# Moving three sets of halved matmuls between chunks, and four VectorE sums to an earlier place, in a fused attention and feed-forward kernel

## The chip, the core and the metric

The kernel runs on one core of a Trainium2 chip. The time is device time in microseconds, the median of several executions. Of the kernel before, 8 executions are known: 280.6 to 282.26 us, median 281.54.

## The reference

A linear attention over 8 batches of 576 tokens with 8 heads of 64 gives 4608 tokens of 512 numbers; a feed-forward layer with a hidden width of 2048 follows.

```python
def _attn_ref(q, k, v):                       # (8, 8, 576, 64) each
    ...
    q_p, k_p = phi(q, cos_w, sin_w), phi(k, cos_w, sin_w)     # relu, times cos and times sin of the position
    kv = np.einsum('bhsf,bhsd->bhfd', k_p, v)
    z = np.sum(k_p, axis=2)
    num = np.einsum('bhsf,bhfd->bhsd', q_p, kv)
    den = np.einsum('bhsf,bhf->bhs', q_p, z)[..., None] + 1e-06
    return (num / den).astype(np.float32)

def _moe_ref(x, w_in, w_out, beta):           # x: (4608, 512)
    h = x @ w_in                              # (4608, 2048)
    g = h * (1.0 / (1.0 + np.exp(-beta * h)))
    return (g @ w_out).astype(np.float32)
```

## The kernel before

The feed-forward part goes over nine chunks (c = 0 to 8) of 512 tokens. For each chunk TensorE forms the hidden values in 16 tiles of 128 (jt), ScalarE takes the swish of each from PSUM into g_t, and TensorE multiplies by w_out. The attention of batch b = c + 1 is laid between the matmuls of chunk c, so that its result (xs, turned by a DMA transpose into xt) is there for the chunks behind. While chunk c runs, the inputs of the next batches are loaded and prepared as well: k_relu and v_scale (on VectorE or ScalarE), q_relu, a DMA transpose of q (q_turn_dma) and q_tan on GpSimd.

Everything is issued in an order written out by hand: each engine executes its instructions in the order in which the code records them, and semaphores keep the engines together. TensorE's list is one straight program. A matmul stands in it as two instructions, a weight load and the matmul itself, which reads up to 512 columns.

Two pieces of the attention are made of very small matmuls, and each of them stands as one unbroken block among the large ones:

- kv_mm (L266, matmul on L272), for both halves of the heads: 72 matmuls of 130 columns, in each chunk up to 6.
- num_mm (L286, matmul on L293), called through num_all (L328) for the three parts of a batch: 144 matmuls of 65 columns. In chunk 1 it is called at slot 18 (one_unit, L818), in chunks 2 to 4 behind h_first (L984), in chunks 5 and 6 at the entry N0 of ORDER.

How the matmuls of the feed-forward part are formed differs from chunk to chunk:

- Chunks 0 and 1: h_group (L410: h_mm, then h_act) for the 16 hidden tiles, then o_part (L530) for the output, four slots for each of four token tiles. o_part has a parameter cols: with 2, each of its matmuls but the very first of a tile is issued as two of half the columns. In chunk 1 this holds for slots 24 to 31 (L833).
- Chunks 2, 3 and 4: h_first (L950) makes the hidden tiles with h_group. The output comes from o_fast (L533): two halves, x and y, of seven products each ("1" to "7"), put together from sums of the g tiles (S1 to S4) and of the weights (T1 to T4) with additions on VectorE (a2, a3, a7) and copies on ScalarE (c1, c5, cu, c4). Each product is eight matmuls of 256 columns; with its last argument set, the last seven are issued as two of 128.
- Chunks 5 to 8: chunk() (L885) walks a list of names, ORDER (L843) for chunks 5 and 6, ORDER_END for 7 and 8. Half of the hidden tiles come in pairs (X, Y, Z, V) from h_fast (L463) in seven products of two matmuls, and eight come plainly as p0 to p7 from h_plain (L419), which also takes cols. Before, H_COLS halves p0 to p7 of chunk 6, and O_COLS halves six of the fourteen output products of chunk 5 (x: 4; y: 2, 5, 7, 3, 4). Both are on L857.

h_fast needs four sums of x, t1 to t4 in the tile wx["x"]. For chunks 6 and later they are the entries t1 to t4 of the lists; for chunk 5 they are made by x_sums (L454) at the end of chunk 4 (L1019), by VectorE. In chunk 4 the end of the code is: y5, c5, v_half, y6, cu, y2, a2, v_half, y7, a7, v_half, y3, a3, v_half, x_sums, v_half, y4, c4. The sums need xt of chunk 5, of which the last part comes from batch 5 (x_part, L992).

Of the kernel before, what the change touches and what calls it, by code (L numbers as in the profile page):

```python
# [16 lines left out]
P = 128  # L17
# [5 lines left out]
def kernel(  # L23
# [14 lines left out]
    nc = tc.nc  # L38
# [5 lines left out]
    MI = DM // P  # L44
# [3 lines left out]
    NB = TCH // 64  # L48
    HP = P // 2
# [319 lines left out]
    def h_bank(c, jt):  # L369
        if c < 2 and jt < 4:  # L370
            return ((3, 2, 5, 0), (6, 7, 4, 5))[c][jt]
        return ((6, 7, 4, 5) if c == 0 else (0, 1, 4, 5))[jt % 4]

    def h_mm(c, jt, mis=range(4), blocks=slice(0, NB)):
        xt = xt_tile(c)
        for mi in mis:
            jp, g = divmod(mi, 2)
            nc.tensor.matmul(ps[:, h_bank(c, jt), blocks.start * 64 : blocks.stop * 64],  # L378
                             lhsT=win[jt // 4][:, mi, (jt % 4) * P : (jt % 4 + 1) * P],
                             rhs=xt[:, blocks, jp, g * HP : (g + 1) * HP],  # L380
                             start=(mi == 0), stop=(mi == MI - 1 and blocks.stop == NB))

    def h_act(c, jt):
        if (c, jt // 4) not in gs:
# [22 lines left out]
        nc.vector.tensor_tensor(T2[:, a], B22[:, a], T1[:, a], op=z)  # L407
        nc.vector.tensor_tensor(T4[:, a], B21[:, a], T2[:, a], op=z)

    def h_group(c, jt):  # L410
        h_mm(c, jt)
        h_act(c, jt)

    def h_silu(c, jt, bank):
# [115 lines left out]
    def o_part(c, tt, part, cols=1):  # L530
        o_mm(c, tt, range(4 * part, 4 * part + 4), cols)

    def o_fast(c, pr, banks, cols=""):  # L533

        b_ps, e_ps, a_ps = (ps[:, k_, 0:HM] for k_ in banks)
        tok = slice(pr * P, (pr + 1) * P)
        last = c == NTC - 1 and pr == 1

        def prod(dst, left, right, start, stop, pieces=False):
            order = (0, 1, 2, 3, 4, 5, 7, 6) if c + 1 >= B else range(JT // 2)  # L540
            for i in order:
                w = HM // 2 if i and pieces else HM
                for m in range(0, HM, w):
                    nc.tensor.matmul(dst[:, m : m + w], lhsT=left(i), rhs=right[:, i, m : m + w],  # L544
                                     start=start and i == 0,
                                     stop=stop and i == order[-1], skip_group_check=True)

        def g_part(r, hf):
            def at(i):
                jt = 2 * i + r  # L550
                return gs[c, jt // 4][:, jt % 4, hf * (TCH // 2) + pr * P : hf * (TCH // 2) + (pr + 1) * P]
            return at

        def s_part(t):
            return lambda i: t[:, i, tok]

        o1 = osb_pool.tile([P, DM], FP32, name="o_sb", tag="o_sb")
        o2 = osb_pool.tile([P, DM], FP32, name="o_sb", tag="o_sb")
        p1 = part.tile([P, HM], FP32, name="p1", tag="p1")
        p5 = part.tile([P, HM], FP32, name="p5", tag="p5")  # L560
        u = part.tile([P, HM], FP32, name="u", tag="u")

        def c4():
            h = HM // 2 if last else HM
            nc.scalar.copy(o2[:, 0:h], b_ps[:, 0:h])
            if last:
                nc.vector.tensor_copy(o2[:, h:HM], b_ps[:, h:HM])
                store(c, pr + 2, o2, 0, HM)

        def stored(key, op):  # L570
            def do():
                op()
                waits[key[0]].discard(key[1:])
                if not waits[key[0]] and not (last and key[0] == "2"):
                    store(c, pr + (2 if key[0] == "2" else 0), o2 if key[0] == "2" else o1)
                if last and key == "2a7":
                    store(c, pr + 2, o2, HM, DM)
            return do

        waits = {"1": {"a2", "a3"}, "2": {"a7", "c4"}}  # L580
        add = dict(op=ALU.add)
        return {
            "1": lambda: prod(b_ps, g_part(0, 0), B11, True, False, "1" in cols),
            "5": lambda: prod(e_ps, s_part(S1), T1, True, False, "5" in cols),
            "6": lambda: prod(b_ps, s_part(S2), T2, False, False, "6" in cols),
            "2": lambda: prod(a_ps, g_part(1, 0), B21, True, True, "2" in cols),
            "7": lambda: prod(b_ps, s_part(S3), T3, False, False, "7" in cols),
            "3": lambda: prod(e_ps, s_part(S4), B22, False, True, "3" in cols),
            "4": lambda: prod(b_ps, g_part(1, 1), T4, False, True, "4" in cols),
            "c1": lambda: nc.scalar.copy(p1, b_ps),  # L590
            "c5": lambda: nc.scalar.copy(p5, e_ps),
            "cu": lambda: nc.scalar.copy(u, b_ps),
            "c4": stored("2c4", c4),
            "a2": stored("1a2", lambda: nc.vector.tensor_tensor(o1[:, 0:HM], a_ps, p1, **add)),
            "a3": stored("1a3", lambda: nc.vector.tensor_tensor(o1[:, HM:DM], e_ps, u, **add)),  # L595
            "a7": stored("2a7", lambda: nc.vector.tensor_tensor(o2[:, HM:DM], b_ps, p5, **add)),
        }
# [231 lines left out]
    for slot in range(32):  # L829
        if slot < 16:  # L830
            h_group(1, slot)
        else:
            o_part(1, (slot - 16) // 4, slot % 4, 2 if slot > 23 else 1)  # L833
        one_unit(slot)

    def k_piece(b, j):
# [20 lines left out]
    H_COLS, O_COLS = {6: 8}, {5: ("4", "25734")}  # L857

    def x_sum(c, kind):
        xt, n = xt_tile(c), NB // 2  # L860
# [24 lines left out]
    def chunk(c, b, x, y, parts):  # L885
# [27 lines left out]
        for op in (ORDER if b < B else ORDER_END).split():  # L913
            n = int(op[-1]) if op[-1].isdigit() else None
            if op == "K":
                kv_mm(b, 0, 4)
                kv_mm(b, 1, 4)
            elif op == "kt":
                kv_take((0, 1), 4)
            elif op[0] == "N":  # L920
                for t, bank in enumerate(parts):
                    num_all(b, t, bank)
            elif op[0] == "x":
                x_part(b, n, parts[n])
                take(op)
            elif op[0] in "kvwq":
                take(op)
            elif op[0] == "t":
                if c + 1 < NTC:
                    x_sum(c + 1, n)  # L930
            elif op[0] == "g":
                if b + 1 < B:
                    q_tan(b + 1, n, None if n else last_sum)
            elif op[0] == "p":
                h_plain(c, plain[n], plain_bank(n), 2 if n < H_COLS.get(c, 0) else 1)
            elif op[:2] == "sp":
                h_silu(c, plain[n], plain_bank(n))
            elif op[0] == "o" and n is not None:
                outs[op[1]][op[2]]()
            elif op[0] == "o":  # L940
                outs[op[2]]["a" + op[1]]()
            elif op[0] == "c" and op[2] in "xyo":
                outs["x" if op[2] == "o" else op[2]][op[:2]]()
            elif op[0] == "s":
                last_sum = g_sum(c, 2 * int(op[1]), 2 * int(op[1]) + 2, n)
            else:
                pair = op[0] if op[0] in pairs else op[-1]
                pairs[pair][op.replace(pair, "")]()

    def h_first(c):  # L950
        b = c + 1
        for slot in range(16):
            h_group(c, slot)
            if c == 2:
                if slot == 0:
                    wx_tiles()
                    k_all(b)
                    v_half(b, 1)
                if slot == 3:
                    att_q(b + 1)  # L960
                if slot == 5:
                    nc.vector.tensor_tensor(T3, B22, B12, op=ALU.subtract)
            if slot == (10 if c == 2 else 1):
                kv_all(b)
            if slot in (3, 7, 11):
                g_sums(c, slot // 2 - 1, slot // 2 + 1)
            elif slot in (13, 15):
                sums = g_sums(c, slot // 2, slot // 2 + 1)
            if c == FAST - 1 and slot in (2, 4, 6, 8, 10, 12):
                wh_sums((0, 4, 8, 12, 2, 6)[slot // 2 - 1])  # L970
        return sums

    FAST = 5
    for c in range(2, NTC):
        b = c + 1
        parts = (6, 0, 4) if c < FAST else (0, 6, 4)
        cols = O_COLS.get(c, ("", ""))
        xb, yb = ((2, 3, 6), (1 if c == FAST - 1 else 7, 3, 6)) if c < FAST else ((3, 2, 0), (1, 2, 0)) if b < B else ((0, 3, 6), (1, 3, 6))
        x, y = o_fast(c, 0, xb, cols[0]), o_fast(c, 1, yb, cols[1])
        if c >= FAST:  # L980
            chunk(c, b, x, y, parts)
            continue
# [21 lines left out]
        v_half(b + 1, 0, 0, 3)  # L1004
        y["5"]()
        y["c5"]()
        v_half(b + 1, 1, 2, 3, "act")
        y["6"]()
        y["cu"]()
# [6 lines left out]
        y["3"]()  # L1016
        y["a3"]()
        v_half(b + 1, 0, 7, 9)
        if c == FAST - 1:  # L1019
            x_sums(c + 1)  # L1020
        v_half(b + 1, 1, 3, 9, "act")
        y["4"]()
        y["c4"]()
# [30 lines left out]
```

## Time and profile before

| what | us |
|---|---|
| median of 8 executions | 281.54 (280.6 to 282.26) |
| the profiled execution | 282.26 |
| its span, first to last instruction | 280.5 |
| TensorE busy | 270.9 |
| VectorE, ScalarE, GpSimd busy | 209.6, 177.9, 71.9 |
| matmuls of num_mm in a chunk, first to last start: chunks 1, 2, 3 | 1.79, 1.68, 2.45 |
| the same, chunks 4, 5, 6 | 1.24, 1.31, 1.30 |

A row of the profile's table of groups gives the line, the engine, the operation, what it writes and reads, how often, the busy time and the mean of one, and then the idle time of the engine before it and what ended most of it ("<-"). "issue" there means that the engine waited for nothing that the profile shows. The chain in order of time gives for each step the start, the length, the engine, the tile and line, and the number of instructions. Durations of single matmuls in the profile overlap, so where it matters the time from one start to the next is used. The granted clock of TensorE is full (1.00) in every ten microseconds but the last (0.91).

### The profile page before, as it was taken

To read this page: it belongs to the slowest core of one execution; us is meant where nothing else is said; L and a number is where in the kernel's file an instruction comes from. 1 tells how busy PE (TensorE), PEld (TensorE's weight loads), DVE (VectorE), ACT (ScalarE), POOL (GpSimd) and SP (SyncE) were. 2 spreads that over 40 slices of the span, in tenths; PEclk is the share of its full clock that TensorE was granted. 3 is DMA by queue.
4 is the path that set the end of the run, shared out by engine and by line. 5 is a ranking of instruction groups with operands and counts; after the bars stand their busy time and mean duration, and the time that the engine had idled before them with its cause. 6 is when DMAs were issued, how large, how long until landed. Compare 5 with 4: busy or idle time off the path is not lost.

```text
span 280.5 us, 8681 instructions
## 1 busy us (share of the span) xinstructions
PE 270.9 (97%) x3586; PEld 192.1 (68%) x3592; DVE 209.6 (75%) x539; ACT 177.9 (63%) x348; POOL 71.9 (26%) x89
## 2 busy tenths in 40 slices
PE   8899999999999999998999999999999999999993
PEld 8454455454674588547854786679888886888783
DVE  5889977659999586356749977799679779649832
ACT  5778856772137557674857585896586169529911
POOL 1444000624194074106320452008400140000000
PEclk9999999999999999999999999999999999999998
DMA  7999999989979959993899189507400540033006
GB/s 235 384 393 380 393 389 299 361 231 398 177 226 324 309 144 255 130 378 52 215 205 367 31 192 229 211 3 119 120 1 5 124 112 1 2 75 78 0 2 150
DMA packets 50583, 53.98 MB, mean 192 GB/s; under 512 B 31200, under 2 KB 31472, under 8 KB 50544
## 3 DMA queue, kind: packets, MB, share of 16 engines
q1 hardware_dynamic: 47584, 45.82, 58.0%
q0 software_dynamic: 2688, 7.34, 9.5%
q8 instruction: 28, 0.46, 0.7%
q10 hardware_dynamic: 272, 0.27, 0.4%
q14 instruction: 11, 0.09, 0.1%
HBM read 36.71 MB, written 9.44 MB: 165 GB/s over the span
## 4 chain that ended last, share of the span: by engine, by line
PE 90%; DMA 3%; DVE 3%; issue 1%; SPq 1%; ACTq 0%; ACT 0%
PE ps L544 30%; PE ps L378 24%; PE ps L472 11%; PE ps L521 10%; PE ps L426 7%; PE ps L293 4%; DMA raw_v<-in_v_dram 3%; PE ps L272 3%; SPq L79 1%; DVE xs L315 1%; DVE vb L219 0%; PE ps L352 0%; PE ps L234 0%; DVE win L115 0%; DVE rden L308 0%
## 5 line engine op out<-in xcount | busy, mean ns | idle before, releaser
L378 PE MATMUL ps<-xt,win 128*128 128x512 bf16 (+1 forms) x324 | 71.1, 377 | 0.1
L386 ACT ACTIVATE g_t<-ps,beta 128x512 bf16<-128x512 f32 x80 | 54.6, 688 | 19.2 <-PE ps L378 17.9
L378 PEld LDWEIGHTS <-win 128*128 128x128 bf16 x324 | 31.1, 98 | 35.4 <-issue 0.4
L514 POOL DMA_DIRECT2D out_dram<-o_sb x56 | 32.7, 590 | 67.0 <-DVE o_sb L595 34.7
L544 PEld LDWEIGHTS <-S 128*128 128x128 bf16 x469 | 44.2, 98 | 4.8
L417 ACT ACTIVATE g_t<-ps,beta 128x512 bf16<-128x512 f32 x64 | 41.2, 696 | 3.4 <-PE ps L426 2.2
L544 PEld LDWEIGHTS <-g_t 128*128 128x128 bf16 x357 | 32.9, 98 | 3.7
L222 POOL TENSOR_TENSOR qs<-qt,tanr 128x1152 bf16<-128x1152 bf16 x8 | 19.0, 2393 | 48.9 <-DVE S L397 17.6
L397 DVE TENSOR_TENSOR S<-g_t 128x512 bf16<-128x512 bf16 (+1 forms) x62 | 22.3, 394 | 11.5 <-ACT g_t L386 9.1
L521 PE MATMUL ps<-wout,g_t 128*128 128x512 bf16 (+1 forms) x152 | 28.4, 337 | 0.5 <-issue 0.3
L544 PE MATMUL ps<-wout,g_t 128*128 128x256 bf16 (+1 forms) x231 | 28.1, 270 | 0.0
L544 PE MATMUL ps<-wout,S 128*128 128x256 bf16 (+1 forms) x238 | 27.4, 266 | 0.0
L544 PE MATMUL ps<-T,S 128*128 128x256 bf16 (+1 forms) x231 | 27.1, 269 | 0.0
L426 PE MATMUL ps<-xt,win 128*128 128x512 bf16 (+1 forms) x120 | 24.0, 336 | 0.0
L315 DVE TENSOR_TENSOR xs<-ps,rden 128x768 bf16<-128x768 f32 (+4 forms) x26 | 22.8, 884 | 0.8
L219 DVE TENSOR_SCALAR vb<-raw_v,cos 128x256 bf16<-128x256 f32 x63 | 22.8, 420 | 0.0
L521 PEld LDWEIGHTS <-g_t 128*128 128x128 bf16 x158 | 15.0, 98 | 11.0
L217 ACT ACTIVATE vb<-raw_v,sin 128x256 bf16<-128x256 f32 (+1 forms) x50 | 21.8, 499 | 0.7 <-DMA raw_v<-in_v_dram 0.7
L472 PE MATMUL ps<-w_stage 128*128 128x256 bf16 x120 | 20.3, 273 | 0.3 <-DVE w_stage L458 0.3
L472 PEld LDWEIGHTS <-w_stage 128*128 128x128 bf16 x160 | 15.5, 98 | 4.2 <-issue 0.5
L222 POOL TENSOR_TENSOR w_stage<-qt,tanr 128x1152 bf16<-128x1152 bf16 x4 | 9.5, 2382 | 26.1 <-DVE den L304 26.1
L426 PEld LDWEIGHTS <-win 128*128 128x128 bf16 x120 | 11.7, 98 | 6.3
(104 smaller groups left out, 384.8 us busy)
## 6 DMA issues: line engine op xcount, KB each, us to landing
raw_v<-in_v_dram SPq DMA_DIRECT2D x7, 1152.0 KB, 11.7
raw_k<-in_k_dram SPq DMA_DIRECT2D x7, 1152.0 KB, 8.5
raw_q<-in_q_dram SPq DMA_DIRECT2D x7, 1152.0 KB, 8.4
out_dram<-o_sb POOLq DMA_DIRECT2D x56, 128.0 KB, 5.3
w_stage<-in_moe_w_in_dram SPq DMA_DIRECT2D x3, 1024.0 KB, 13.6
w_stage<-in_moe_w_out_dram SPq DMA_DIRECT2D x2, 1024.0 KB, 7.8
w_stage<-in_moe_w_out_dram SPq DMA_DIRECT2D x4, 512.0 KB, 12.1
out_dram<-o_sb SPq DMA_DIRECT2D x13, 128.0 KB, 2.4
```

The costliest lines, as they stand in the source:

```text
L219: nc.vector.tensor_scalar(o, a, scalar1=t[:, n : n + 1], scalar2=None, op0=ALU.mult)
L222: return eng.tensor_tensor(dst.rearrange("q n (g p) -> q n g p", g=2), src.rearrange("q n (g p) -> q n g p", g=2), tanr[:, n0:n1].unsqueez ...
L315: nc.vector.tensor_tensor(o.rearrange("q j n s d -> q j (n s) d"), nv[:, :, a:z, :, 0:D].rearrange("q j n s d -> q j (n s) d"), rden[:, :, ...
L378: nc.tensor.matmul(ps[:, h_bank(c, jt), blocks.start * 64 : blocks.stop * 64], lhsT=win[jt // 4][:, mi, (jt % 4) * P : (jt % 4 + 1) * P], ...
L386: nc.scalar.activation(gs[c, jt // 4][:, jt % 4], ps[:, h_bank(c, jt)], AF.Silu, scale=beta[:, jt : jt + 1])
L397: return nc.vector.tensor_tensor(o, l, r, op=op)
L417: nc.scalar.activation(gs[c, jt // 4][:, jt % 4], ps[:, bank], AF.Silu, scale=beta[:, jt : jt + 1])
L426: nc.tensor.matmul(ps[:, bank, o * 64 : z * 64], lhsT=win[jt // 4][:, mi, (jt % 4) * P : (jt % 4 + 1) * P], rhs=xt[:, o:z, jp, g * HP : (g ...
L472: nc.tensor.matmul(dst, lhsT=left[:, g], rhs=right[:, :, g * HP : (g + 1) * HP], start=start and g == 0, stop=stop and g == 1, skip_group_ ...
L514: eng.dma_start(out=out_v[bb, n][:, m0:m1], in_=o_sb[hf * HP : (hf + 1) * HP, m0:m1])
L521: nc.tensor.matmul(o_ps[:, m0 : m0 + w], lhsT=gs[c, jt // 4][:, jt % 4, tt * P : (tt + 1) * P], rhs=wout[:, jt, m0 : m0 + w], start=(jt == ...
L544: nc.tensor.matmul(dst[:, m : m + w], lhsT=left(i), rhs=right[:, i, m : m + w], start=start and i == 0, stop=stop and i == order[-1], skip ...
```

## The change

Four things change. In chunk 1, o_part halves its matmuls from slot 19 on instead of from slot 24. H_COLS and O_COLS give way to one table, SPLITS, which has for a chunk the number of hidden tiles (the first ones) and of output products (the last ones in the order in which they are made) that are halved: one hidden tile in chunk 3, eight output products in chunk 4, and p0 to p4 in chunk 5. h_mm and h_group get the parameter cols for this, and late(c) counts the output products of a chunk as they are made. So chunk 6 no longer halves its hidden tiles, and chunk 5 none of its output products. Last, x_sums of chunk 5 moves up in chunk 4's code, from behind y3, a3 and a v_half to behind y5 and c5. In all, 27 matmuls and 27 weight loads more are issued; what is computed stays the same.

```diff
-    def h_mm(c, jt, mis=range(4), blocks=slice(0, NB)):
+    def h_mm(c, jt, mis=range(4), blocks=slice(0, NB), cols=1):
         xt = xt_tile(c)
         for mi in mis:
             jp, g = divmod(mi, 2)
-            nc.tensor.matmul(ps[:, h_bank(c, jt), blocks.start * 64 : blocks.stop * 64],
-                             lhsT=win[jt // 4][:, mi, (jt % 4) * P : (jt % 4 + 1) * P],
-                             rhs=xt[:, blocks, jp, g * HP : (g + 1) * HP],
-                             start=(mi == 0), stop=(mi == MI - 1 and blocks.stop == NB))
+            w = (blocks.stop - blocks.start) // (cols if mi > mis[0] else 1)
+            for i in range(blocks.start, blocks.stop, w):
+                nc.tensor.matmul(ps[:, h_bank(c, jt), i * 64 : (i + w) * 64],
+                                 lhsT=win[jt // 4][:, mi, (jt % 4) * P : (jt % 4 + 1) * P],
+                                 rhs=xt[:, i : i + w, jp, g * HP : (g + 1) * HP],
+                                 start=(mi == 0), stop=(mi == MI - 1 and i + w == NB))
...
-    def o_fast(c, pr, banks, cols=""):
+    made = {}
+
+    def late(c):
+        made[c] = made.get(c, 0) + 1
+        return made[c] > 14 - SPLITS.get(c, (0, 0))[1]
+
+    def o_fast(c, pr, banks):
...
-            "1": lambda: prod(b_ps, g_part(0, 0), B11, True, False, "1" in cols),
+            "1": lambda: prod(b_ps, g_part(0, 0), B11, True, False, late(c)),
...
-            o_part(1, (slot - 16) // 4, slot % 4, 2 if slot > 23 else 1)
+            o_part(1, (slot - 16) // 4, slot % 4, 2 if slot > 18 else 1)
...
-    H_COLS, O_COLS = {6: 8}, {5: ("4", "25734")}
+    SPLITS = {3: (1, 0), 4: (0, 8), 5: (5, 0)}
...
-                h_plain(c, plain[n], plain_bank(n), 2 if n < H_COLS.get(c, 0) else 1)
+                h_plain(c, plain[n], plain_bank(n), 2 if n < SPLITS.get(c, (0, 0))[0] else 1)
...
-            h_group(c, slot)
+            h_group(c, slot, 2 if slot < SPLITS.get(c, (0, 0))[0] else 1)
...
         y["5"]()
         y["c5"]()
+        if c == FAST - 1:
+            x_sums(c + 1)
         v_half(b + 1, 1, 2, 3, "act")
...
         v_half(b + 1, 0, 7, 9)
-        if c == FAST - 1:
-            x_sums(c + 1)
         v_half(b + 1, 1, 3, 9, "act")
         y["4"]()
         y["c4"]()
```

More of the change, by code (lines that the diff above doesn't have):

```diff
@@ L408, in w_sums, with h_group @@
         nc.vector.tensor_tensor(T4[:, a], B21[:, a], T2[:, a], op=z)
-    def h_group(c, jt):
-        h_mm(c, jt)
+    def h_group(c, jt, cols=1):
+        h_mm(c, jt, cols=cols)
         h_act(c, jt)
@@ L582, in o_fast @@
         return {
-            "1": lambda: prod(b_ps, g_part(0, 0), B11, True, False, "1" in cols),
[L584 to L589, printed above, removed]
+            "1": lambda: prod(b_ps, g_part(0, 0), B11, True, False, late(c)),
+            "5": lambda: prod(e_ps, s_part(S1), T1, True, False, late(c)),
+            "6": lambda: prod(b_ps, s_part(S2), T2, False, False, late(c)),
+            "2": lambda: prod(a_ps, g_part(1, 0), B21, True, True, late(c)),
+            "7": lambda: prod(b_ps, s_part(S3), T3, False, False, late(c)),
+            "3": lambda: prod(e_ps, s_part(S4), B22, False, True, late(c)),
+            "4": lambda: prod(b_ps, g_part(1, 1), T4, False, True, late(c)),
             "c1": lambda: nc.scalar.copy(p1, b_ps),
@@ L976 @@
         parts = (6, 0, 4) if c < FAST else (0, 6, 4)
-        cols = O_COLS.get(c, ("", ""))
         xb, yb = ((2, 3, 6), (1 if c == FAST - 1 else 7, 3, 6)) if c < FAST else ((3, 2, 0), (1, 2, 0)) if b < B else ((0, 3, 6), (1, 3, 6))
-        x, y = o_fast(c, 0, xb, cols[0]), o_fast(c, 1, yb, cols[1])
+        x, y = o_fast(c, 0, xb), o_fast(c, 1, yb)
         if c >= FAST:
```

## The prediction

> **What bounds the kernel now.** First the busy rows of the page and the chain that ended last: TensorE is busy 97% of the span and carries 90% of the chain, so only TensorE time counts, either matmul streaming or gaps between matmuls.
>
> ```profile
> PE 270.9 (97%) x3586; PEld 192.1 (68%) x3592; DVE 209.6 (75%) x539; ACT 177.9 (63%) x348; POOL 71.9 (26%) x89
> ...
> q8 instruction: 28, 0.46, 0.7%
> ...
> PE 90%; DMA 3%; DVE 3%; issue 1%; SPq 1%; ACTq 0%; ACT 0%
> ```
>
> Streaming is nearly incompressible: in the trace a 256-wide matmul starts 109.2 ns after the one before it, a 512-wide one 216 ns. So I looked for gaps: the table of waits from 60 to 270 us, then the chain in order of time.
>
> ```profile
> PEld L293 <- issue: 4.1, 9, 1.1
> ...
> PE ps L293 <- issue: 1.7, 3, 1.0
> ```
>
> ```profile
> 125.99 1.25 PE ps L293 x122
> 127.24 1.03 issue
> 128.57 12.33 PE ps L544 x112
> ...
> 155.97 1.36 PE ps L293 x137
> 157.32 10.49 PE ps L544 x96
> ```
>
> (Columns: us in total, times, the longest.) L293 is num_mm: 144 tiny matmuls with 144 weight loads in one burst per chunk. Three of the bursts hold a pause in which nothing that the profile names is awaited ("issue"). From first to last matmul start, the bursts of chunks 1, 2 and 3 take 1.79, 1.68 and 2.45 us, that of chunk 4 takes 1.24 us with no pause. So the pauses cost 0.55, 0.44 and 1.21 us.
>
> What are they? Queue q8 carried 28 packets of 16,384 bytes, and 7,208 TensorE instructions over 28 is about 256 to a packet (64 bytes each): TensorE's own instructions. I counted the built program's TensorE instructions in order. The first instruction after each pause has number 1987, 2754 and 3523; every 256th from 195 gives 1987, 2755, 3523. So the pauses stand at block boundaries, and each ends a constant time after the start of the last packet on q8:
>
> ```
> burst of chunk   boundaries in or before it   packet starts   pause ends   difference
> 1                17 before, 239 inside             67.30          69.88        2.58
> 2                25 inside, 281 inside             95.89          98.37        2.48
> 3                 8 inside, 264 inside            125.75         128.27        2.52
> 4                 9 before, 247 inside            153.86     no pause (next block needed 3.08 later)
> 6                15 before, 241 inside            210.58     no pause (3.09 later)
> ```
>
> I read it so: crossing one boundary starts the fetch of the block that begins 256 instructions later, and this is usable 2.5 us after its packet starts. Ordinary code needs 14 to 28 us for 256 instructions, a burst some 1.3 us. **A burst that lies over two boundaries stalls; one that lies over one, with the other well ahead of it, doesn't.** Another gap is of another kind:
>
> ```profile
> 169.50 0.38 PE L472 MATMUL ps<-xt,win 128*128 128x256 bf16 x2
> 170.23 0.38 PE L472 MATMUL ps<-w_stage 128*128 128x256 bf16 x2 [0.35 <-DVE w_stage L458]
> ```
>
> At the start of chunk 5 product X5 waits for the first sum of x_sums. Start to start it is 623 ns where 109 is normal: 0.51 us.
>
> **The change part by part.** *Splits.* A halved matmul adds one weight load and one matmul. Chunk 1 gains 19 (parts 19 to 23 of its output), chunk 3 3 (slot 0), chunk 4 56 (its last 8 output products), chunk 5 15 (p0 to p4) and loses 42 (output products), chunk 6 loses 24: +27 net, 54 instructions. Their price is in the timeline, where chunk 5 has both forms (192.80 and later are split):
>
> ```profile
> 191.06 1.04 PE L544 MATMUL ps<-T,S 128*128 128x256 bf16 x8
> 191.93 1.04 PE L544 MATMUL ps<-wout,S 128*128 128x256 bf16 x8
> 192.80 1.05 PE L544 MATMUL ps<-wout,g_t 128*128 128x256 bf16 x15
> 193.69 1.05 PE L544 MATMUL ps<-T,S 128*128 128x256 bf16 x15
> 194.59 1.05 PE L544 MATMUL ps<-wout,S 128*128 128x256 bf16 x15
> ```
>
> Unsplit products follow each other in 0.87 us, split ones in 0.89: seven splits for 0.0175 us, 2.5 ns each, with all weight loads hidden. 27 x 2.5 ns = **+0.07 us**. Halved h_mm (L378, chunk 0) and h_plain (L426, chunk 6) show the same 2.5 ns.
>
> *Where the boundaries fall.* Counted in the changed program the bursts' numbers give:
>
> ```
> burst of chunk    before: boundaries      after
> 1                 17 before, 239 in       the same (the new splits come behind it)
> 2                 25 in, 281 in           13 before, 243 in
> 3                  8 in, 264 in           36 before, 220 in
> 4                  9 before, 247 in       53 before, 203 in
> 5                 182 in                   4 before, 252 in
> 6                 15 before, 241 in       187 in
> ```
>
> Chunk 1 keeps its 0.55. Chunk 2: h matmuls ahead of the burst run at 0.108 us an instruction, so a boundary 38 instructions further forward is crossed up to 4.1 us sooner, about 91 to 92. How long a request then waits varies: behind the three pauses, where the crossing is known, the next packet starts 2.75, 1.16 and 1.59 us later. So the packet starts about 93 to 95.5, the block is usable at 95.5 to 98, and is needed at about 97.7: **-0.44 us**, at worst +0.3 (a packet 4 us late). Two rows are near: chunk 1 (17 before, and a pause; its packet 1.03 us behind the boundary's weight load) and chunk 4 (9 before, none, 0.57 us to spare, with the DMA at 1.01 to 1.08 just ahead). I go by chunk 4, which has chunk 2's code, h_first, in front. Chunk 3: 44 instructions sooner, 4.7 us, so usable by about 124 to 126 against a need at about 127: **-1.21 us**. Chunk 4 only gains room. Chunk 6 needs one block in its burst, asked for long before: 0 as now.
>
> Chunk 5 is the unknown. Its boundary moves to the first weight load of V4, four ahead of the burst, and the next is 252 inside. TensorE's fetch runs ahead of the array: in chunk 6, now, the packet starts 1.03 us before the boundary's own weight load, and 0.66 us after the sum (a3 of pair Z) that the matmul two before the boundary waits for. In chunk 5 that sum ends at 181.73, the matmul that waits for it is seven before the boundary, so the packet starts at 182.4 to 182.8 and the block is usable at 184.9 to 185.3; its first instruction is wanted at 185.51. Cost 0; above, if the fetch were only asked for once V4's own wait (a7V, 183.4) is over, 3.6 us later is 187.0: +1.5 us. Below nothing isn't possible, since this burst has no pause now. I take **0**, by the nearest row (chunk 6), and keep +1.5 for the range.
>
> *x_sums of chunk 5 moved up.* Its four operations (169.75 to 171.31, 1.56 us) now follow the v_scale that ends at 165.42. VectorE is idle from there to 167.13:
>
> ```profile
> 164.56 0.86 DVE L219 TENSOR_SCALAR vb<-raw_v,cos 128x256 bf16<-128x256 f32 x3
> 167.13 0.42 DVE L594 TENSOR_TENSOR o_sb<-ps,p 128x256 f32<-128x256 f32 x1 [1.71 <-ACT vb L217]
> ```
>
> 1.56 fits into 1.71, so what was queued behind (a2 of y, then v_scale, a7, a3) starts no later than 0.05 us either way. Its input is there: the transpose it waits for landed at 161.84. It issues no DMA and adds no wait. If the idle stretch were shut, a2 to a3 would come up to 1.56 us later, and Y1 of chunk 5, which overwrites the bank that a3 reads (169.31 against 169.50), with them. With the sums done, X5 follows Y1 at once; next late is X6, whose copy c1X then ends near 170.7 while p0 keeps TensorE until 171.0. **-0.51 us** (0 if something else in that stretch holds X5).
>
> **Sum:** -0.44 - 1.21 - 0.51 + 0.07 = -2.09 us on the profiled execution's 282.26: 280.17. That execution is the highest of the eight (280.6 to 282.26), 0.72 above the median 281.54. If its surplus is longer pauses, a median run gains less, 1.4; if not, 2.1. Between 279.45 and 280.17 I take **279.6**.
>
> [...]
>
> **Rivals.**
> *The pauses aren't the fetch, or return at other boundaries* (they fall wherever 288 instructions run short): only x_sums counts, 281.1. For: no view names a releaser. Against: three of three at boundaries, three equal differences. 0.09.
> *Chunk 5's burst stalls* by about 1.5: 281.1 as well, -0.6 (and down to 280.3 at 0.7). For: 0.2 us to spare. Against: chunk 6. 0.12, half of it still beyond 0.3%.
> *Slower: the fetch has no lead.* If a packet starts only 1.1 us (quiet DMA) to 3.2 us (as the one at 172.19, that long after its boundary's weight load) after the boundary is executed, chunk 5 (V4 at 184.06) has its block at 187.7 to 189.8, 2.2 to 4.3 late, and chunk 2 (boundary near 95.0) at 98.6, 0.9 late, 0.45 more than now. -1.21 - 0.51 + 0.07 + 0.45 + 2.2 to 4.3 = +1.0 to +3.1: 282.5 to 284.6. It decides once chunk 5's pause exceeds 2.1 us. Against: nine of the 28 packets start ahead of the boundary's weight load. 0.06.
>
> The forecast itself: 0.73, its own range 278.8 to 280.5. Range for 8 in 10: 278.8 to 281.1. What a measurement of this kernel can tell from no change is 0.3%, 0.84 us. Faster (below 280.7): 0.73 + half of 0.12 = 0.79; same: 0.09 + the other half = 0.15; slower 0.06.
>
> **What would show it.** Waits of L293 for "issue": one left, near 69.3, of chunk 1. The burst of chunk 3 is 1.24 us long instead of 2.45, that of chunk 2 1.24 instead of 1.68, that of chunk 5 unchanged at 1.31. q8 still 28 packets. X5 110 ns behind Y1, x_sums between v_scale and a2 with no new idle behind. Wrong if a burst of chunk 2, 3 or 5 holds a pause, or Y1 comes late.

## The result, and the profile after

The changed kernel takes 280.3 us (median of 11 executions, 279.88 to 280.88); the kernel before, timed beside it, 281.68 (32 executions). The ratio is 0.9954, 95% interval 0.9939 to 0.9969: faster by 0.46%, some 1.3 us. 279.6 had been forecast, with 278.8 to 281.1 as the range.

The profiled execution took 280.55 us, its span 278.7 where before it was 280.5. The first rows of the page:

```profile
PE 271.5 (97%) x3613; PEld 193.5 (69%) x3619; DVE 209.6 (75%) x539; ACT 177.8 (64%) x348; POOL 70.7 (25%) x89
...
q8 instruction: 28, 0.46, 0.7%
...
PE 86%; DMA 9%; DVE 2%; SPq 1%; issue 1%; ACTq 0%; ACT 0%
```

27 matmuls and 27 weight loads more, and still 28 packets of instructions. TensorE bounds the time as before. (The DMA's larger share of the chain is one step, the load of q from 24.61 to 39.60 us, through which the chain is followed back in this execution; TensorE is busy in that stretch as it was before, 14.8 of the 15 us from 25 to 40 us in both.)

The table of waits from 60 to 270 us has lost the row "PE ps L293 <- issue", and L293's weight loads wait less:

```profile
PEld L293 <- issue: 1.9, 6, 0.4
```

The chain in order of time shows the bursts of chunks 2, 3 and 4:

```profile
96.86 1.16 PE ps L293 x109
98.02 0.12 issue
98.14 0.38 PE ps L293 x22
98.53 12.33 PE ps L552 x112
...
125.93 1.36 PE ps L293 x135
127.29 12.33 PE ps L552 x112
...
154.69 1.36 PE ps L293 x138
156.05 12.47 PE ps L552 x168
```

(L552 is the former L544.) Chunk 3's chain had 1.03 us of "issue" inside the burst, ahead of its last matmuls; now the burst runs through to the products and looks like chunk 4's. In chunk 2 some of the pause is left: at 98.02 the chain has "issue", and the last 22 matmuls of the burst follow from 98.14 on.

The start of chunk 5, VectorE and then TensorE, from the timeline:

```profile
163.28 0.86 DVE L219 TENSOR_SCALAR vb<-raw_v,cos 128x256 bf16<-128x256 f32 x3
164.06 0.41 DVE L460 TENSOR_TENSOR w_stage<-xt 128x512 bf16<-128x512 bf16 x1
164.51 0.43 DVE L461 TENSOR_TENSOR w_stage<-xt,w_stage 128x512 bf16<-128x512 bf16 x1
164.85 0.42 DVE L462 TENSOR_TENSOR w_stage<-xt 128x512 bf16<-128x512 bf16 x1
165.18 0.42 DVE L463 TENSOR_TENSOR w_stage<-xt,w_stage 128x512 bf16<-128x512 bf16 x1
165.94 0.42 DVE L602 TENSOR_TENSOR o_sb<-ps,p 128x256 f32<-128x256 f32 x1 [0.34 <-ACT vb L217]
```

```profile
168.36 0.38 PE L474 MATMUL ps<-xt,win 128*128 128x256 bf16 x2
168.58 0.38 PE L474 MATMUL ps<-w_stage 128*128 128x256 bf16 x2
168.80 0.38 PE L474 MATMUL ps<-xt,win 128*128 128x256 bf16 x2
169.01 1.03 PE L428 MATMUL ps<-xt,win 128*128 128x512 bf16 x7
```

The four sums fill the old idle stretch and leave 0.34 us of it, a2 behind them isn't late, and X5 starts 0.22 us behind the first of Y1's two matmuls, the plain pace (0.73 before).

From the starts of the matmuls, the two profiled executions differ as follows (burst lengths from first to last start):

```
                                    before    after    difference
start of chunk 1's burst             68.31    68.91      +0.60   (the instructions up to here are the same)
burst of chunk 1                      1.79     1.24      -0.55
burst of chunk 2                      1.68     1.55      -0.13
burst of chunk 3                      2.45     1.24      -1.21
bursts of chunks 4, 5, 6    1.24, 1.31, 1.30   1.24, 1.31, 1.31    0
X5 behind Y1                          0.62     0.11      -0.51
27 matmuls more                                          +0.07
sum                                                      -1.73   (spans: -1.74)
```

### The profile page after: what moved, and what is told of

Same layout as the page of the kernel before. It is cut to its first block, busy times and chain, and to the rows that moved or that the text cites. A ratio compares the mean times of both kernels' runs of the same rounds, so it can differ in the third digit from the quotient of the medians.

```text
span 278.7 us, 8735 instructions
## 1 busy us (share of the span) xinstructions
PE 271.5 (97%) x3613; PEld 193.5 (69%) x3619; DVE 209.6 (75%) x539; ACT 177.8 (64%) x348; POOL 70.7 (25%) x89
## 4 chain that ended last, share of the span: by engine, by line
PE 86%; DMA 9%; DVE 2%; SPq 1%; issue 1%; ACTq 0%; ACT 0%
PE ps L552 31%; PE ps L380 22%; PE ps L474 11%; PE ps L523 8%; PE ps L428 7%; DMA raw_q<-in_q_dram 5%; PE ps L293 4%; DMA raw_v<-in_v_dram 3%; PE ps L272 2%; DVE xs L315 1%; SPq L79 1%; PE ps L234 0%; PE ps L352 0%; DVE win L115 0%; DVE qb L194 0%
## 5 line engine op out<-in xcount | busy, mean ns | idle before, releaser
L516 POOL DMA_DIRECT2D out_dram<-o_sb x56 | 31.6, 571 | 66.0 <-DVE o_sb L603 33.2
L552 PEld LDWEIGHTS <-S 128*128 128x128 bf16 x476 | 44.3, 98 | 4.8
L552 PEld LDWEIGHTS <-g_t 128*128 128x128 bf16 x364 | 33.0, 98 | 3.6
L523 PE MATMUL ps<-wout,g_t 128*128 128x256 bf16 (+1 forms) x171 | 28.6, 318 | 0.4 <-issue 0.2
L552 PE MATMUL ps<-wout,g_t 128*128 128x256 bf16 (+1 forms) x238 | 28.1, 267 | 0.0
L552 PE MATMUL ps<-wout,S 128*128 128x256 bf16 (+1 forms) x238 | 27.4, 266 | 0.0
L552 PE MATMUL ps<-T,S 128*128 128x256 bf16 (+1 forms) x238 | 27.1, 266 | 0.0
L523 PEld LDWEIGHTS <-g_t 128*128 128x128 bf16 x177 | 16.9, 98 | 9.2
```

Of the source, the lines that this page charges most:

```text
L516: eng.dma_start(out=out_v[bb, n][:, m0:m1], in_=o_sb[hf * HP : (hf + 1) * HP, m0:m1])
L523: nc.tensor.matmul(o_ps[:, m0 : m0 + w], lhsT=gs[c, jt // 4][:, jt % 4, tt * P : (tt + 1) * P], rhs=wout[:, jt, m0 : m0 + w], start=(jt == ...
```

## Experiments

**The sums alone, and the splits alone.** The first is the kernel before with this edit, the second the changed kernel with it taken back:

```diff
         y["c5"]()
+        if c == FAST - 1:
+            x_sums(c + 1)
...
         v_half(b + 1, 0, 7, 9)
-        if c == FAST - 1:
-            x_sums(c + 1)
```

> The kernel before with only x_sums of chunk 5 moved up; every TensorE instruction keeps its number. My theory (two separate gains): X5 follows Y1 by about 110 ns instead of 623, so 0.5 us less than before; the bursts of chunks 2 and 3 keep boundaries 25 and 8 inside and stay long (about 1.6 and 2.4 us). Rival (the moved sums are paid back by a2, a3 or by X6): Y1 or X6 comes late by as much and the time is within 0.1 us of before. Rival 2 (the sums are the whole gain): 1.4 us less than before.

> The changed kernel with x_sums at its old place. My theory: the bursts of chunks 2 and 3 take about 1.55 and 1.24 us as in the changed kernel, the gap of 0.5 us at X5 is back; 0.9 us less than before, 0.5 more than the changed kernel. Rival (sums are the whole gain): the time of before, or 0.07 more.

The sums alone: ratio to before 0.9981 (0.9964 to 0.9998), 281.05 us. The splits alone: 0.9982 (0.9969 to 0.9994), 280.83 us, with X5 605 ns behind Y1 again. The two gains are 0.37% together, against 0.46% for the whole change, so within the intervals they add up; neither is the whole. The sums gave what was expected (0.19% is 0.54 us). The splits gave 0.5 us by the ratio, with an interval of 0.2 to 0.9, where 0.9 was expected; the medians differ by 0.91 (281.74 to 280.83). And the profile of the sums alone had a surprise: with every TensorE instruction at its old number, the bursts of chunks 2 and 3 took 1.43 and 1.38 us, not 1.6 and 2.4. The pauses were in their places, but small.

**How much do the pauses of the kernel before vary?** Two more profiles of it, nothing edited:

> The kernel before once more, for a second profile of it. My theory after the first four runs: the place of a boundary decides whether a pause can come, the start of the packet how long it is; so the bursts of chunks 2 and 3 are between 1.24 and 2.5 us long, not always 1.68 and 2.45, and the pause of chunk 3 is on average about half of the 1.21 us of the first profile. Rival: 1.68 and 2.45 within 0.1 again, and the single look with the sums alone (1.43 and 1.38) was an exception.

> The kernel before, a third profile; expected as for the second.

With the first profile and that of the sums alone, whose TensorE instructions have the same numbers, these make four profiles of one layout, and there are five of the layout of the changed kernel in chunks 1 to 4 (within 6 instructions; e3, e5 and e6 are further down). A pause is what a burst takes over 1.24 us. The last column says how long before the burst's first matmul the start of the last packet on queue q8 lay, by the DMA records of the trace:

```
layout of before      chunk 1   chunk 2   chunk 3   packet ahead of chunk 3's burst
first profile           0.55      0.44      1.21      0.17
e7                      0.14      0.41      0.72      0.58
e8                      0.13      0.98      0.39      0.89
e1 (sums alone)         0         0.19      0.14      1.14
mean                    0.20      0.51      0.62

layout of after
after                   0         0.31      0         3.43
e2 (splits alone)       0         0         0         3.64
e3                      0         0.13      0         3.10
e5                      0         0         0         3.25
e6                      0         0         0         3.25
mean                    0         0.09      0
```

The pause of chunk 3 shrinks as the packet (that of the block which begins inside the burst) starts earlier: 0.17, 0.58, 0.89 and 1.14 us ahead of the burst go with 1.21, 0.72, 0.39 and 0.14, a sum of 1.28 to 1.38 each time. That block begins 264 instructions into the burst, some 1.14 us at 288 in 1.24 us (an estimate), so from packet to use it is 2.4 to 2.5 us in each of the four. So in these nine profiles the place of the boundary decided whether there could be a pause in chunk 3, and the start of the packet how long it was. The first profile held the longest pause of the four in chunk 3; the two new ones, 0.72 and 0.39, are about half of it, as was expected. In the waits of the second profile the pauses are smaller rows:

```profile
PEld L293 <- issue: 3.1, 8, 0.6
...
PE ps L293 <- issue: 0.8, 2, 0.5
```

**Chunk 1's splits alone.**

```diff
-            o_part(1, (slot - 16) // 4, slot % 4, 2 if slot > 23 else 1)
+            o_part(1, (slot - 16) // 4, slot % 4, 2 if slot > 18 else 1)
```

> The kernel before with only the splits of chunk 1 from slot 19 on: 19 matmuls more, all behind the burst of chunk 1; H_COLS, O_COLS and x_sums as before. Counted, the bursts then have their boundaries: chunk 2 13 before and 243 in, chunk 3 30 before and 226 in, chunk 4 47 before, chunk 5 144 in, chunk 6 53 before and 203 in. My theory: no burst but that of chunk 2 pauses; chunk 3's burst 1.24 us; the same time as the splits alone (0.9 less than before). So the splits of chunks 3, 4 and 5 do nothing for the time. Rival (the splits near a burst are what helps, those of chunks 3 to 5): chunk 3's burst stays at 2.4 us or chunk 5 or 6 pauses, and the time is that of before.

The ratio to before is 0.9973 (0.9959 to 0.9987), the median 280.73 us, and the bursts of chunks 3 to 6 take 1.24, 1.24, 1.31 and 1.30 us. As far as the intervals tell, nineteen matmuls far ahead of the bursts do all that the splits do, and the other splits of the change add nothing.

**Without the splits of chunks 4 and 5.**

```diff
-    SPLITS = {3: (1, 0), 4: (0, 8), 5: (5, 0)}
+    SPLITS = {3: (1, 0)}
```

> The changed kernel without the splits of chunks 4 and 5: 71 matmuls fewer. Boundaries: chunks 1 to 4 as in the changed kernel, chunk 5 138 in, chunk 6 73 in, with the next one 329 in, 41 instructions behind the end of the burst. My theory: chunk 5 has no pause, chunk 6 one of 0 to 0.3 us some 41 instructions behind its burst; against the 0.18 us saved the time is that of the changed kernel within 0.15. Rival (the splits of 4 and 5 are needed, as the bursts of chunks 5 and 6 are placed by them): a pause of over 1 us in chunk 5 or 6 and 1 us more.

The ratio is 0.9952 (0.9933 to 0.9970), the median 280.33 us, as for the changed kernel (0.9954), and no burst of chunks 1 to 6 holds a pause, nor is there one behind chunk 6's. So 71 of the splits in the changed kernel are not needed, and its placing of the bursts of chunks 5 and 6 gains nothing: without it they lie well too.

**A pause put where there was none.** If the account by positions is right, a pause can be made to order, and its instruction named beforehand:

```diff
-    SPLITS = {3: (1, 0), 4: (0, 8), 5: (5, 0)}
+    SPLITS = {3: (1, 0), 4: (0, 8), 5: (5, 10)}
```

> The changed kernel with ten more output products of chunk 5 halved, behind its burst: 70 matmuls, 140 instructions more, all between the bursts of chunks 5 and 6. Only chunk 6 is moved: its burst had a boundary 187 in, now 47 in, and the next one 303 in, that is 15 instructions behind its end, at the eighth matmul of the product that follows. My theory: the boundary is crossed as the burst begins, the packet starts 1.1 us later and the block is usable 2.5 us after that, 3.6 us into the burst, where the eighth matmul would be due after 2.1; so TensorE stands still there, for 'issue', for 1.2 to 1.5 us, with hardly any DMA running, and the time rises by 1.4 to 1.7 us (0.18 of it for the 70 matmuls). Rival (the pauses come from the DMA load, or the splits are harmless wherever they lie): no pause in or behind the burst of chunk 6, 0.18 us more than the changed kernel.

The median is 281.81 us, 1.5 more than the changed kernel's 280.3; the ratio to before is 1.0021 (1.0004 to 1.0039), so the whole gain is lost (by the two ratios 1.9 us). The timeline of TensorE behind the burst of chunk 6:

```profile
211.40 0.22 PE L293 MATMUL ps<-kv,qs 64*64 64x65 bf16 x4
211.56 0.94 PE L552 MATMUL ps<-wout,g_t 128*128 128x256 bf16 x7
213.82 0.28 PE L552 MATMUL ps<-wout,g_t 128*128 128x256 bf16 x1 [1.33 <-issue]
213.94 1.91 PE L552 MATMUL ps<-T,S 128*128 128x256 bf16 x16
```

Seven of the product's eight matmuls run, then TensorE stands for "issue", and the eighth starts 1,600 ns behind the seventh instead of 109. The packet had started at 211.11, 2.71 us ahead. The place was named to the instruction and the length (1.49 us) lies within the expected one; the DMA is nearly idle there (share 0.00 to 0.08 from 208 to 214 us). So this pause came with hardly any DMA load, and the splits were not harmless there.

**All of chunk 1 halved.**

```diff
-            o_part(1, (slot - 16) // 4, slot % 4, 2 if slot > 18 else 1)
+            o_part(1, (slot - 16) // 4, slot % 4, 2 if slot > 15 else 1)
```

> The changed kernel with all output parts of chunk 1 halved (from slot 16 on): 11 matmuls more, 22 instructions, ahead of the burst of chunk 1. Boundaries then: chunk 1 39 before and 217 in (17 and 239 in the changed kernel), chunk 2 35 before and 221 in (13 and 243), chunk 3 58 before, chunk 4 181 in, chunk 5 26 before, chunk 6 165 in. My theory: the packet of chunk 2 starts before the stretch from 93 us on in which the 256-byte packets of the turned q run, its block is there in time, and the 0.3 us that are left of its pause go; chunk 1 can't pause either. 0.3 to 0.5 us less than the changed kernel. Rival (the packet is held up by the turned q wherever the boundary lies, or the lead is bounded): the pause of chunk 2 stays at 0.3 us, time of the changed kernel plus 0.03.

> The kernel with all of chunk 1 halved, a second look: by the theory on the turned q its packet starts again within or behind the 256-byte packets, 1.3 to 1.8 us ahead of the burst.

The ratio is 0.9953 (0.9938 to 0.9969), the median 280.26 us: no better than the changed kernel. The expectation failed twice. In the first profile the burst of chunk 2 took 1.24 us, so its pause is gone, but by the five profiles above only 0.09 us on average was left to gain, not 0.3. And the packet didn't move with the boundary: its boundary's weight load was issued at 92.87, 2.3 us sooner than in the changed kernel (95.19), but the packet started at 95.16 against 95.50. The second profile was of an execution that ran late from the start (283.69 us, chunk 1's burst at 70.60): here the packet started at 98.67, 4.1 us behind its boundary's weight load, and the burst of chunk 2 took 2.97 us although its boundary lay 35 ahead:

```profile
98.62 1.07 PE ps L293 x107
99.69 1.55 issue
...
101.71 12.33 PE ps L552 x112
```

Between 93 and 97 us (95.4 to 101.0 in the late one) the DMA records show the 2,304 packets of 256 bytes with which q is turned.

**The turn of q moved.** On top of the kernel with all of chunk 1 halved:

```diff
-                if slot == 3:
+                if slot == 11:
                     att_q(b + 1)
```

> As the kernel with all of chunk 1 halved, but in chunk 2 the relu and the DMA transpose of the next q stand behind hidden tile 11 instead of 3, some 7 us later. It measures what holds up the instruction packet of chunk 2: in the six profiles with a boundary 13 or 35 ahead of the burst it started between 1.29 and 1.69 us before the burst, whether the boundary's weight load was 0.3 or 2.3 us older. Theory (the 256-byte packets of the turned q, 93 to 96 us, hold it up): with these behind it the packet starts within 1 us of the boundary's weight load, at 93.9 or before, 3 us or more ahead of the burst. Rival (the large loads of k and v, which keep the DMA at 1.0 from 86 to 93, hold it up, or the request is made late): it starts near 95 again, 1.3 to 1.8 us ahead of the burst. The time isn't judged.

> The same kernel with the later turn of q, a second look, expected as for the first: theory packet 3 us or more ahead of the burst, rival 1.3 to 1.8 us.

In the two profiles the packet started at 93.09 and 92.89, 0.24 and 0.02 us behind its boundary's weight load (92.85, 92.87) and 3.7 and 4.0 us ahead of the burst. The packets of the turned q now ran from 95.8 to 98.8. The loads of k and v before them were where they had been:

```profile
83.83 0.37 SPq L79 DMA_DIRECT2D raw_k<-in_k_dram  x1
86.20 0.37 SPq L79 DMA_DIRECT2D raw_v<-in_v_dram  x1
94.65 2.68 SPq L252 DMA_TRANSPOSE qt<-qb  x1
```

Of these only the transpose (SP's third line, issued at 87.4 with q turned early) has moved; q's relu ahead of it moved with it, and so did the load of the next q behind it (94.5 to 97.4), which comes after the wait had begun either way. So with the boundary 35 ahead it was the turned q that held up the instruction packet, by 2.1 to 2.3 us (95.16 against 93.09 and 92.89). Whether it does so in the changed kernel, where the boundary lies 13 ahead, wasn't tried: there the packet starts 0.31 us behind its boundary's weight load, hardly more than here. With the turn away the burst still takes 1.34 to 1.35 us. The remaining 0.1 is not explained: its largest gap, 0.09 us, stands ahead of the 96th matmul, and not at the boundary, which is at the 111th.

## Why the prediction was right, and where it was off

**The mechanism** was right as far as the runs show it: the pauses stand at block boundaries, on the count of every 256th TensorE instruction from number 195 (before, the first instructions after them were 1987, 2754 and 3523, against 1987, 2755 and 3523 by the count). Every pause of more than 0.12 us inside a burst of L293, in all the profiles, ends at such a number or at the weight load just ahead of it, and the one made to order did too. And where the pages of before and after count 28 instruction packets, that of the kernel with 140 instructions more counts 29.

**Its signs.** No pause of chunk 1 is left, where one was forecast to stay. And the text called itself wrong if a burst of chunk 2, 3 or 5 held a pause: chunk 2's did in the profiled execution (0.31 us), though in three of the other four profiles of that layout there is none.

**Price of the splits.** 2.5 ns each, +0.07: nothing in the runs speaks against it; 71 splits fewer (0.18) are below what the intervals can tell (280.33 against 280.3).

**Chunk 5, "I take 0".** Right. The packet started at 180.79, 0.65 us after the sum that p7 waits for (180.14) and 2.0 us ahead of the burst, just as chunk 6's row had it; the burst took 1.31 us. **Chunks 4 and 6:** 0, as said.

**The sums, -0.51.** Right: 0.62 to 0.11 in the profile, and 0.54 us (0.06 to 1.0) when moved alone.

**Chunk 3, -1.21.** The pause went in all five profiles, but the term was mis-sized: 1.21 was read off one execution, the slowest of the eight, and there the packet was late. The mean of four profiles is 0.62. The prediction saw that this execution stood 0.72 us above the median and moved the forecast by part of that; it should have asked what its pauses would be in the others.

**Chunk 2, -0.44.** About right on average (0.51 to 0.09), but by luck, since the reason was wrong. The step "a boundary 38 instructions further forward is crossed up to 4.1 us sooner" failed. The boundary's weight load came 1.60 us sooner (96.79 before, 95.19 in the changed kernel): of the 38 instructions 25 stood inside the burst, where one takes some 4 ns (288 in 1.24 us), so for the weight loads the pace of 0.108 us holds for 13 alone. And the packet came only 0.39 us sooner (95.89, then 95.50), at the late end of the forecast 93 to 95.5. The gain came from a smaller step than forecast: the packet started 1.29 to 1.54 us ahead of the burst in the five profiles of the new layout, 0.32 to 0.97 in the four of the old. The prediction did not look for the turned q, whose packets run there from 93.12 to 97.12; how much of the delay in the changed kernel is due to them stays open, as said above.

**Chunk 1, "keeps its 0.55".** Wrong for a profile: 0.20 on average before, 0 in all five after, though nothing up to that burst is changed. Why the packet there starts 1.6 to 2.0 us ahead of the burst in the profiles after, and 1.0 to 1.9 in those before, stays open.

With the means, -0.62 - 0.42 - 0.51 + 0.07 is -1.48, and -1.68 with chunk 1's 0.20; the medians differ by 1.38, and the ratio gives 0.9 to 1.7. The forecast's -2.09 was too much by chunk 3's 0.59. The forecast time of 279.6 is 0.7 us below the measured 280.3, and the error would have been larger by 0.20 without chunk 1's gain, which nothing in the change explains.

**The first rival**, that only the sums count, stood at 281.1, 0.8 us above the measured 280.3. Most crossings gave no pause inside the bursts of chunks 1 to 6: of 28, at most three did. But the pauses of chunks 2 and 3 were what the splits were worth.

## What to carry to other kernels

A pause for "issue" in a run of tiny matmuls is worth a count of instructions: if it stands, as here, at every 256th, the loading of code is the first thing to suspect, and a few more instructions well ahead of the run may move it away (here 19 matmuls in chunk 1, for a ratio of 0.9973); here they didn't have to be near. A single profile shows where such a pause is, not how long it is on average: take three or four before its length goes into a sum. And after any edit that adds or removes instructions ahead of such a run, count again, as the same edit can bring a pause where there was none (70 matmuls more: +1.5 us).

## What the runs showed of the hardware that was not expected

- The instruction packet of chunk 2 was held up by other DMA traffic. With the 256-byte packets of a DMA transpose in its way and all of chunk 1 halved it started 2.29 us after its boundary's weight load, and 4.1 us in the late execution; with the transpose moved, 0.24 and 0.02 us. Large loads are no clear contrast: they keep the DMA as busy in chunk 3 (share 1.01 to 1.08 from 119 to 123 us), where the packet started 0.23 to 0.73 us behind it in all five profiles of that layout, but in the kernel before the second to fourth packet (18.57, 24.73 and 41.65 us), all ahead of the first 256-byte one (42.3), started 2.8 to 3.9 us behind at a share of 1.04 to 1.06 (10 to 50 us). What decides the wait is not shown.
- From the packet's start to the first use of the block it took 2.25 to 2.7 us in all pauses, of which the packet itself took 0.95 to 1.4.
- In the split products of chunk 5 in the kernel before, 128-wide matmuls, each with its own weight load of 98 ns (as the profile times it), follow each other at 55.8 ns.
